# Attention denominators summed over partitions by accumulating DMAs and a small VectorE sum, in place of products with ones

## The chip, the cores and the metric

The kernel runs on one core of a Trainium2 chip. The metric is the device time of one execution in microseconds (us), lower being better. Every time below is a median of several executions. An execution is called slow when it is over 1.5% above the fastest of the same kernel. Each kernel with changes was run on the same chip and in the same rounds as the kernel before.

## The reference, cut to what matters

```python
B, H, S, D = 4, 8, 768, 64               # 16 clusters, d_model = H * D = 512
def attention(q, k, v, centroids):       # per batch and head
    q_assign = argmax(cos(q, centroids)); k_assign = argmax(cos(k, centroids))
    mask = q_assign[:, None] == k_assign[None, :]
    scores = where(mask, q @ k.T / sqrt(D), -1e9)
    e = exp(scores - max(scores))
    return (e / (sum(e) + 1e-9)) @ v
def hyena(x):                            # x: heads concatenated, [B, S, 512]
    x1, x2, x3 = split(x @ w_proj)
    y = x1 * irfft(rfft(x2, axis=1) * rfft(filter_fft, axis=0), axis=1) * x3
    return y @ w_out
```

`sum(e)` is the denominator that this case is about. The output is float32, [4, 768, 512].

## The kernel before

Work is done in 16 "head pairs" (two heads of one batch). For each of six key tiles of 128 keys TensorE makes scores, ScalarE turns them into `p` (exp), TensorE adds `p` times v into `pair`, and VectorE adds `p` into an accumulator `acc`, 128 partitions by 1,536. The keys lie on the partitions, so at the end of a head pair `acc` must still be summed over its 128 partitions. The kernel before does that with products with a block of ones, in four 32-column quadrants of the TensorE array:

```python
def den(e):
    for hp in range(2):
        for ch in range(2):
            z = 2 * hp + ch
            T.nc.tensor.matmul(ap(h)[32 * z:32 * z + 32, :384], T.ones32, T.acc[:, hp, ts(ch, 384)],
                               start=True, stop=True)
op(("PE", .68), den, te + 0.5, r=["acc", "ones"], w=[h], alloc=h, kind="den")
op(EV384, lambda e: copy(e, T.den, ap(h)[:, :384]), te + 1.5, r=[h], w=["den"], free=[h])
# 12 columns on each partition, by way of DRAM; then 1/x; then broadcast to all partitions
op(("SP", .6), ... dma_start(T.dd[os], T.den[0:128:32]), te + 2, r=["den"], w=[("dd", os)], byts=6e3)
op(("SP", .6), ... dma_start(T.dn, T.dd[os] ...), te + 4, r=[("dd", os)], w=["dn"], byts=6e3)
op(("DVE", .52), rec, te + 6, r=[], w=["dn"])                       # + eps, reciprocal
op(("SP", .6), ... dma_start(T.dr[os] ..., T.dn), te + 7, r=["dn"], w=[("dr", os)], byts=6e3)
for hp in range(2):
    op(("SP", .6), ... dma_start(T.rb[64 * hp:64 * hp + 64], T.dr[os][hp:hp + 1].to_broadcast([64, S])), te + 9, ...)
op(("DVE", 1.05), ... scalar_tensor_tensor(osv(), osv(), eps(), rbv(), ...), te + 12, ...)     # normalise
op({"ACT": .83, "DVE": .55}, ... copy(e, T.xT[xs][:, kt] ..., osv()), te + 13, ...)            # cast to bf16 xT
```

`xT` is what the projections of `hyena` read, so the whole chain from `den` to `xT` sets when they can start.

The code does not issue instructions directly. It makes a list of operations, each with an engine, a *modelled* duration, its inputs and a "due" time. A planner then simulates them and fixes one order for each engine, in which its instructions are issued. If an operation's input comes later than the model thought, the engine waits there, with everything planned after it: in the trace after (below) VectorE stood 6.59 us before one normalisation, and behind that ScalarE 4.90 and TensorE 4.52.

The softmax here doesn't subtract the row's maximum and nothing guards it: scores larger than these inputs give would overflow.

## Time and profile before

The kernel before takes 403.2 us (three executions, 401.54 to 403.23).

| | before |
|---|---|
| TensorE busy, share | 380.2 us, 95% |
| VectorE busy, share | 370.1 us, 92% |
| ScalarE busy, share | 275.5 us, 69% |
| share of TensorE in the chain that ended last | 81% |
| products with ones | 128 instructions |
| waits of the normalisation for its broadcast | 0.3 us |

First the page of its profile: the span, the busy time of each engine with its share of the span and its number of instructions, the granted TensorE clock and the DMA busy share in tenths for 40 slices of the span, the line of the software DMA queue (packets, MB, share of the 16 engines), and the chain of work that ended last.

```profile
span 401.3 us, 8872 instructions
PE 380.2 (95%) x3498; PEld 209.2 (52%) x3498; DVE 370.1 (92%) x513; ACT 275.5 (69%) x522; POOL 16.8 (4%) x55
...
PEclk9999999999999999999999999999999999999988
DMA  9939968127411433126521326014212001100304
...
q0 software_dynamic: 1056, 2.10, 3.0%
...
PE 81%; DVE 11%; ACT 4%; issue 2%; POOL 0%; DVEq 0%; POOLq 0%; ACTq 0%
```

TensorE (PE) is busy 95% and VectorE (DVE) 92%: two engines near their limit, with 21.1 us of TensorE idle in the whole span (401.3 − 380.2). Now some groups of instructions: line, engine, operation, tiles, shapes and count, then busy us and mean ns of one, then the engine's idle time just before them and what ended it.

```profile
L732 PE MATMUL bank<-acc,ones 128*32 128x384 f32 x128 | 13.6, 498 | 0.2 <-DVE acc L719 0.2
L780 DVE SCALAR_TENSOR_TENSOR osb<-osb,rb 128x768 f32<-128x768 f32 x15 | 15.2, 1013 | 0.3 <-DMA rb<-dr 0.3
L279 DVE CAST xT<-osb 128x768 bf16<-128x768 f32 x15 | 8.4, 560 | 0.5
```

The products with ones are 128 instructions. The normalisation (L780) waited 0.3 us for its broadcast in the whole run: the denominator chain is hidden. The timeline shows how well, for one head pair (start, duration, engine, line, operation). The reciprocal is followed at once by other work, and the normalisation comes 12.8 us later with no wait before it (there is no bracket at its end):

```profile
67.70 0.23 DVE L744 RECIPROCAL dn<-dn 128x12 f32<-128x12 f32 x1
...
80.54 1.01 DVE L780 SCALAR_TENSOR_TENSOR osb<-osb,rb 128x768 f32<-128x768 f32 x1
```

Finally the view by stretches of time, here two of its stretches: length, then busy us (and instructions) of PE, PE weight loads, DVE, ACT and POOL, then clock, DMA busy share and GB/s.

```profile
60.00:100.00 40.00, 39.08 (x322) 21.04 (x318) 34.95 (x40) 34.21 (x67) 0.00 (x0) 1.00 0.51 124
...
300.00:330.00 30.00, 29.93 (x280) 16.03 (x276) 29.44 (x40) 19.53 (x38) 0.00 (x0) 1.00 0.09 22
```

TensorE works almost without a gap in both, and the DMA engines have room, 0.51 and 0.09.

### The profile page before, as it was taken

The page shows a single profiled execution, that of the slowest core. Times are in us where ns is not written, and L with a number is a line of the kernel's source. Part 1 is how long each engine was busy: PE and PEld are TensorE (multiplying, and loading weights), DVE is VectorE, ACT ScalarE, POOL GpSimd, SP SyncE. Part 2 cuts the span into 40 slices and gives each one's busy share as a digit, 9 for nine tenths or more (in the row PEclk, how much of TensorE's full clock was granted, in tenths as well). Part 3 has the DMA queues.
Part 4 walks back from the last instruction along what each step waited for, and adds up shares of the span by engine and source line. Part 5 has one row for each costly group of instructions (what it writes and reads, how often), then busy time and mean ns, then how long its engine had stood idle before and what let it go on. Part 6 is the DMA issues. An engine that isn't in the chain of part 4 may idle for free.

```text
span 401.3 us, 8872 instructions
## 1 busy us (share of the span) xinstructions
PE 380.2 (95%) x3498; PEld 209.2 (52%) x3498; DVE 370.1 (92%) x513; ACT 275.5 (69%) x522; POOL 16.8 (4%) x55
## 2 busy tenths in 40 slices
PE   3979999999999999999999999999999999999963
PEld 2544554645545655554545655564555555555731
DVE  8899997989899999999899999997999999999981
ACT  4997888889855897676872877689865676523512
POOL 8700000000000000000000000000000000000000
PEclk9999999999999999999999999999999999999988
DMA  9939968127411433126521326014212001100304
GB/s 173 228 59 219 210 145 199 41 65 193 123 43 27 117 76 86 43 82 196 135 84 57 80 47 153 3 41 167 94 41 51 10 3 42 42 2 20 140 0 158
DMA packets 67233, 37.09 MB, mean 92 GB/s; under 512 B 56700, under 2 KB 62328, under 8 KB 67192
## 3 DMA queue, kind: packets, MB, share of 16 engines
q1 hardware_dynamic: 62856, 33.62, 32.5%
q0 software_dynamic: 1056, 2.10, 3.0%
q10 hardware_dynamic: 3280, 0.82, 1.2%
q8 instruction: 27, 0.44, 0.4%
q14 instruction: 14, 0.11, 0.1%
HBM read 30.66 MB, written 6.48 MB: 93 GB/s over the span
## 4 chain that ended last, share of the span: by engine, by line
PE 81%; DVE 11%; ACT 4%; issue 2%; POOL 0%; DVEq 0%; POOLq 0%; ACTq 0%
PE bank L63 30%; PE pair L709 29%; PE bank L817 5%; PE bank L674 4%; PE bank L570 3%; PE bank L732 3%; PE bank L599 3%; DVE acc L719 2%; PE bank L467 1%; PE bank L610 1%; ACT p L698 1%; DVE y L907 1%; PE bank L493 1%; DVE hm L454 1%; DVE yy L905 1%
## 5 line engine op out<-in xcount | busy, mean ns | idle before, releaser
L709 PE MATMUL pair<-p,vraw 128*64 128x385 f32 x768 | 143.3, 489 | 0.0
L698 ACT ACTIVATE p<-bank 128x512 f32<-128x512 f32 x192 | 114.2, 617 | 29.6 <-PE bank L63 25.3
L719 DVE TENSOR_TENSOR acc<-p,acc 128x1536 f32<-128x1536 f32 x64 | 111.9, 1748 | 4.0 <-ACT p L698 2.4
L709 PEld LDWEIGHTS pair<-p,vraw 128*64 128x64 f32 x768 | 53.6, 136 | 44.6 <-issue 37.9
L63 PE MATMUL bank<-aug,aug 128*64 128x512 bf16 (+3 forms) x610 | 69.1, 326 | 1.4 <-DVE aug L536 0.7
L695 ACT ACTIVATE p<-bank 128x512 f32<-128x512 f32 x96 | 58.8, 612 | 4.2 <-PE bank L63 3.1
L63 PE MATMUL bank<-xT,wpj 128*64 128x384 bf16 x512 | 51.9, 327 | 0.1
L63 PEld LDWEIGHTS <-aug 128*64 128x64 bf16 (+1 forms) x610 | 35.3, 109 | 30.2 <-issue 17.5
L63 PEld LDWEIGHTS <-wpj 128*64 128x64 bf16 x512 | 27.9, 109 | 22.3 <-issue 13.5
L277 ACT COPY qkT<-bank 128x384 f32<-128x384 f32 x58 | 27.2, 497 | 10.3 <-PE bank L63 9.3
L63 PEld LDWEIGHTS <-y 128*64 128x64 bf16 x448 | 22.4, 112 | 18.3 <-issue 6.9
L719 DVE TENSOR_TENSOR acc<-p,p 128x1536 f32<-128x1536 f32 x16 | 28.0, 1752 | 1.8 <-ACT p L698 1.5
L674 PE MATMUL bank<-aug,aug 80*128 80x256 bf16 (+1 forms) x120 | 28.6, 274 | 0.0
L63 PE MATMUL bank<-wout,y 128*64 128x512 bf16 x192 | 25.4, 402 | 3.3 <-DVE y L907 3.3
L841 DVE TENSOR_TENSOR tm<-bank,hm 128x512 f32<-128x512 f32 x44 | 27.7, 680 | 0.0
L570 PE MATMUL bank<-ident,qkraw 128*128 128x128 f32 x144 | 27.1, 275 | 0.0
L277 ACT CAST aug<-qkT 64x768 bf16<-64x768 f32 x30 | 24.9, 831 | 1.6 <-DVE qkT L279 1.0
L817 PE MATMUL bank<-wpj,xT 128*64 128x512 bf16 x192 | 22.1, 379 | 1.0 <-DVE xT L279 1.0
L277 ACT COPY ob<-bank 128x512 f32<-128x512 f32 x20 | 11.5, 589 | 15.0 <-PE bank L63 14.8
L570 PEld LDWEIGHTS bank<-ident,qkraw 128*128 128x128 f32 x144 | 18.3, 141 | 3.8 <-issue 2.1
L279 DVE CAST aug<-qkT 64x768 bf16<-64x768 f32 x30 | 16.6, 552 | 2.4 <-ACT qkT L277 1.7
L724 ACT COPY osb<-pair 128x770 f32<-128x770 f32 x16 | 12.8, 800 | 8.6 <-PE pair L709 8.3
(145 smaller groups left out, 436.8 us busy)
## 6 DMA issues: line engine op xcount, KB each, us to landing
vraw<-in_v_dram SPq DMA_DIRECT2D x16, 384.0 KB
qkraw<-in_q_dram SPq DMA_DIRECT2D x30, 192.0 KB
qkraw<-in_k_dram SPq DMA_DIRECT2D x30, 192.0 KB
rb<-dr SPq DMA_DIRECT2D x30, 192.0 KB
out_dram<-ob SPq DMA_DIRECT2D x11, 512.0 KB
y<-in_moe_filter_fft_dram SPq DMA_DIRECT2D x4, 384.0 KB
wpj<-in_moe_w_proj_dram POOLq DMA_DIRECT2D x1, 1536.0 KB, 12.8
aug<-ohT SPq DMA_DIRECT2D x60, 24.0 KB
```

The source lines that it names most:

```text
L63: tensor.matmul(out[64 * i:64 * i + 64], lhsT[:, 64 * i:64 * i + 64], rhs, start=start, stop=stop)
L277: T.nc.scalar.copy(out, in_)
L279: (T.nc.vector if e == "DVE" else T.nc.gpsimd).tensor_copy(out, in_)
L570: tr2 = [lambda i=i, s=s, h=h: T.nc.tensor.transpose(bank(h.ids[i // 3])[:, ts(i % 3, 128)], raw(s, i), T.ident) for i in range(NT)]
L674: T.nc.tensor.matmul(ap(h)[:, c:c + hi - lo], ag[1][:K, ts(sk, 128)], ag[0][:K, lo:hi], start=True, stop=True)
L695: T.nc.scalar.activation(o, ap(h).rearrange("p (a b) -> p a b", a=2), Act.Exp, scale=0.125)
L698: T.nc.scalar.activation(flat(s)[:, lo:lo + 512], ap(h), Act.Exp, scale=0.125)
L709: T.nc.tensor.matmul(o[64 * hp:64 * hp + 64, ch, :385], T.vraw[vs][:, hp, sk * D:(sk + 1) * D], T.p[slots[sk]][:, hp, 384 * ch:384 * ch + ...
L719: T.nc.vector.tensor_tensor(T.acc[:], P_(t[0]), P_(t[1]) if len(t) == 2 else T.acc[:], op=Alu.add)
L724: op(("ACT", .83), lambda e: T.nc.scalar.copy(T.osb[os], two(ob)[:, :, :385]), te, r=[ob], w=[("osb", os)], free=[ob])
L817: T.nc.tensor.matmul(ap(h)[64 * i:64 * i + 64], T.xT[xs][:, kt, c:c + 64], T.wpj[:, kt, DM:2 * DM], start=kt == 0, stop=kt == ND - 1)
L841: op(("DVE", .68), lambda e, i=i, cs=cs, r=r, h=h: T.nc.vector.tensor_tensor(T.tm[r][:, cs], ap(h), hmrow(i, (0, 2, 2, 3)[2 * r + cs]), op ...
```

## The change

The intent is to take the 128 products with ones off the busiest engine and give the sum over partitions to the DMA engines, which have room. For the first 14 of 16 head pairs three DMAs issued by GpSimd add the upper half of the partitions onto the lower half (64, then 32, then 16 rows of 6 KB). The 16 rows that remain are written to DRAM and read back so that each partition holds 12 columns of all 16 rows. One small VectorE reduction adds the 16. The accumulator is doubled, so that the next head pair can start.

The diff (541 lines), cut to its core. Cuts are marked with `...`.

```diff
-        h = Bank()
-        def den(e):
-            ... products with ones ...
+        late = n == NG - 1                       # the last two head pairs keep the products
...
+                flat_ = lambda: T.acc[os][:].rearrange("p a b -> p (a b)")
+                rows = 64
+                while rows >= ROWS:              # ROWS = 16
+                    op(("POOL", 1.0), lambda e, rows=rows: T.nc.gpsimd.dma_start(
+                        flat_()[:rows], flat_()[rows:2 * rows], accum_op=Alu.add), te, r=[], w=[("acc", os)],
+                       byts=rows * 12e3)
+                    rows //= 2
+                op(("SP", .6), ... dma_start(T.dd[os], flat_()[:ROWS]), te + 2, r=[("acc", os)],
+                   w=[("dd", os)], byts=98e3)
+                op(("SP", .6), ... dma_start(T.dp, T.dd[os].rearrange("r (p b) -> p r b", b=12)),
+                   te + 4, r=[("dd", os)], w=["dp"], byts=700e3)
+                def gather(e):
+                    T.nc.vector.tensor_reduce(T.dn, T.dp[:].rearrange("p r b -> p b r"), axis=AX, op=Alu.add)
+                    T.nc.vector.tensor_scalar(T.dn, T.dn, EPS * S, None, op0=Alu.add)
...
# the normalisation writes bf16 xT itself; the cast is gone
-            op(("DVE", 1.05), ... scalar_tensor_tensor(osv(), osv(), eps(), rbv(), ...
-        op({"ACT": .83, "DVE": .55}, lambda e: copy(e, T.xT[xs][:, kt]..., osv()), ...
+            op(("DVE", .6 if last else 1.05), ... scalar_tensor_tensor(xv()[:, a_], osv()[:, a_], eps(), ...
...
# products may use all 128 columns if the array is in that mode already; scores no longer woven with transposes
-MODES = {"pv": (64, 64), "score": (64, 64), "bc": (64, 64), "inv": (64, 64), "proj": (64, 64), ...
+MODES = {"pv": 64, "bc": 64, "half": 64, "sim": 32, "den": 32, "score": 0, "proj": 0, "inv": 0}
...
# the planner: a bandwidth for each queue instead of one for all; loads not before due - LEAD; new constants
-                s = max(o.end + 1.3, st.bw)
-                st.bw = s + o.byts / rate
-                o.end = st.bw + 0.6
+                s = max(o.end + 1.3, st.bw.get(e, 0.0))
+                st.bw[e] = s + o.byts / rate
+                o.end = st.bw[e] + 0.6
...
-    T0 = 10.36
-    TAU1 = 3.298
+    T0 = 9.692
+    TAU1 = 3.059
```

So the diff has two parts: the denominators, and "the rest": the direct write of `xT`, the array modes, the unwoven scores and the planner's changes.

## The prediction

> **What bounds the kernel.** The busy-time lines give TensorE 380.2 us of 401.3 (95%), VectorE 370.1 (92%), ScalarE 275.5 (69%). By stretches, from 60 to 350 us TensorE is busy 98 to 100%, VectorE 87 to 99%. The chain of waits is TensorE 81%, VectorE 11%. From 340.9 to 389.4 us the timeline shows VectorE without a gap: the tail is VectorE's. DMA is busy 83 to 93% until 60 us and 10 to 50% later.
>
> **Removed.** (1) 14 of 16 products with ones. In the TensorE timeline each lasts 0.78 us to the next start, and the group before takes 0.10 us longer than usual (1.40 after 1.30), since the array changes from 64 to 32 columns: 14 x 0.88 = 12.3 us. [...] (2) 14 denominator evictions: about 5 us ScalarE, 1 VectorE. (3) The normalisation writes bf16 xT directly; 16 casts go: 8.4 us VectorE, 0.8 ScalarE. (4) Scores woven with transposes. I count this as nothing: 3 scores with 6 transposes took 1.42 us woven; apart they take 0.65 + 0.80. (5) Score and projection products may stay in 128-column mode after a transpose: perhaps 5 to 20 of 124 mode changes saved, 0.5 to 2 us.
>
> **Added.** For 14 head pairs, three accumulating DMAs (64, 32, 16 partitions of 6 KB) issued by GpSimd, a 98 KB write, a read back in 48-byte pieces (2,048), and a VectorE reduction of 192 elements. A reduction of 384 took 0.555 us, so I estimate 0.36 us, 5 us in all. The accumulator is doubled. I guess a latency of 30 to 40 us to the normalisation; projections that need xT are placed later and the accumulator is rewritten only after some 25 us, so mostly it hides. [...] the trace has no accumulating DMA, so its speed is my largest unknown.
>
> **Critical path.** TensorE falls by about 13 us (380 to 367), nearly all in its saturated stretch. VectorE falls by 4 to 5 us (to about 365), ScalarE by 6. VectorE becomes co-limit and returns some of the gain; work that either engine may do will shift to ScalarE. I expect attention to end (last accumulation, 348.9 + 1.75 us) 7 to 9 us earlier, and the tail to shorten by 2 to 4 us, because more of the third batch's convolution fits before it and a cast leaves its chain. In sum about 11 to 12 us.
>
> **Predicted: 391.5 us, 8 in 10 between 385 and 399. Faster by over 2%: 0.76; within 2%: 0.20; slower: 0.04.**
>
> **What would show it.** Products with ones fall from 128 instructions to 16; TensorE busy 364 to 370, VectorE 362 to 368, both 92% or more of the span; no xT cast; a reduction group of about 0.36 us x14; the woven 256-column scores gone, some score products with 128 columns; software-queue packets up; no long wait of accumulator additions on a DMA; mode changes under 124.
>
> **What would make it wrong.** Accumulating DMAs slower than about 6 us each: the accumulator or xT comes late and TensorE waits. The software queue slowing VectorE, or delaying input loads before 100 us. VectorE already being the true limit, so that only 4 or 5 us come. Whole 128-column products slower than pairs of halves.

## More of the kernel before

The model of a DMA in the kernel before has one bandwidth for all queues:

```python
if o.byts:                              # a DMA
    s = max(o.end + 1.3, st.bw)         # st.bw: when the DMA engines are free, all queues together
    st.bw = s + o.byts / rate
    o.end = st.bw + 0.6
```

## The result

The changed kernel takes 423.0 us (four executions, 421.83 to 424.82) against 403.22 in the same rounds. The ratio is 1.0505, with a 95% interval from 1.0458 to 1.0551: slower by 5%. The predicted 391.5 us, and even the upper end of the range, 399, are far off. Ratios here and below are the mean time of one kernel's fast runs over that of the other's of the same rounds, so they are not quite the ratio of the medians quoted.

The page of the profile after:

```profile
span 421.4 us, 8556 instructions
PE 380.4 (90%) x3312; PEld 212.4 (50%) x3312; DVE 366.8 (87%) x507; ACT 276.4 (66%) x512; POOL 50.0 (12%) x95
...
PEclk9979999996999999999999999999996999989988
DMA  9939989858966984649985772454856211101203
...
q0 software_dynamic: 3296, 11.73, 19.7%
...
PE 52%; DVE 23%; DMA 13%; issue 5%; ACT 3%; SPq 2%; ACTq 1%; DVEq 0%
```

Three things are to be seen. First, TensorE is busy as long as before to within 0.2 us, although it runs 186 instructions fewer. Second, the clock line has new dips, a 7, two 6s and an 8 in the first 36 slices. Third, the chain that ended last is no longer a TensorE chain. DMA is 13% of it, and it was not in the list before.

TensorE's idle time grew from 21.1 to 41.0 us (421.4 − 380.4), by 19.9, which is the whole loss of 20.1 us of span. The removed work is there: counted from the trace's instructions, the products with ones fell from 10.2 to 1.3 us, and changes of array mode fell from 124 to 83, which at the prediction's 0.10 us each is 4.1 us (in the trace before, 8 products of `p` and v take 1.30 us to the next start when that product has 64 columns, 1.40 when it has 128 and 1.43 when it has 32: medians of 61, 17 and 12 groups). But there are 23.9 us of half clock between 15 and 385 us; before there was none. TensorE was busy for 18.4 us of them and so did 9.2 us less work, an estimate from half the rate: in one group of 8 products of `p` and v at half clock, the starts came 276 ns apart, at full clock 143 (median of 92 groups). The slow clock takes back most of the saving (−8.9 − 4.1 + 9.2 = −3.8; measured +0.2; where the other 4.0 us went was not separated), and the idle time comes on top.

Where does it arise? Groups of the profile after, with the idle time before them at the end:

```profile
L765 DVE SCALAR_TENSOR_TENSOR xT<-osb,rb 128x768 bf16<-128x768 f32 x15 | 15.2, 1014 | 11.4 <-DMA rb<-dr 11.2
L688 ACT COPY osb<-pair 128x770 f32<-128x770 f32 x16 | 12.8, 802 | 13.9 <-DVE xT L765 9.1
L729 DVE TENSOR_REDUCE dn<-dp 128x12 f32<-128x192 f32 x14 | 6.8, 485 | 0.0
```

The normalisation now waits 11.2 us for its broadcast `rb` (0.3 before). ScalarE in turn waits 9.1 us for the normalisation, because the copy out of `pair` needs the buffer `osb` that the normalisation reads. The view by stretches shows two places where this hurts:

```profile
60.00:100.00 40.00, 30.84 (x240) 15.44 (x236) 29.45 (x36) 29.48 (x55) 4.94 (x6) 0.97 0.77 140
...
300.00:330.00 30.00, 25.17 (x206) 13.73 (x204) 21.61 (x22) 19.17 (x37) 3.88 (x5) 0.89 0.60 104
```

From 60 to 100 us TensorE lost 8.2 us of busy time against before, from 300 to 330 it lost 4.8. The DMA share rose from 0.51 to 0.77 and from 0.09 to 0.60. The timeline of the second place shows a stall running through three engines (the bracket is the idle time before, and what ended it; SPq is the issue of a DMA on SyncE):

```profile
305.16 5.09 SPq L449 DMA_DIRECT2D aug<-ohT  x6
310.34 0.52 SPq L733 DMA_DIRECT2D dr<-dn  x1
310.91 1.14 SPq L449 DMA_DIRECT2D aug<-ohT  x2
314.02 1.12 SPq L736 DMA_DIRECT2D rb<-dr  x2
...
320.70 1.02 DVE L765 SCALAR_TENSOR_TENSOR xT<-osb,rb 128x768 bf16<-128x768 f32 x1 [6.59 <-DMA rb<-dr]
321.75 0.80 ACT L688 COPY osb<-pair 128x770 f32<-128x770 f32 x1 [4.90 <-DVE xT L765]
321.77 2.35 PE L795 MATMUL bank<-wpj,xT 128*64 128x512 bf16 x10 [4.52 <-DVE xT L765]
```

Read it from the top. The reciprocal was done at 308.78. Its write `dr` (L733) was issued only at 310.34, behind six mask copies issued before it on the same queue (305.16 to 310.25). The broadcasts `rb` went out from 314.02, beside a 64-row accumulate issued at 314.41, and the second landed at 320.6. The normalisation waited 6.59 us, ScalarE 4.90, TensorE 4.52. The clock was at half from 319.4 to 326.2 us. TensorE was busy for 4.4 us of that, so at half the rate it lost another 2.2 us of work. The granted clock in the intervals at half is 0.5, elsewhere 1.0, and between 15 and 385 us they last 3.4 or 6.8 us. How long TensorE must stand idle for one to come is not shown. At 319.4 us TensorE had stood idle for 2.1 us only, and in d_noacc (below) half clock at 65.8 us followed a gap of 1.79 us, while a gap of 2.74 us here, at 65.6 us, brought none.

The list of DMA issues has the new transfers (queue, count, KB each, median us from issue to landing):

```profile
acc<-acc POOLq DMA_DIRECT2D x14, 384.0 KB, 5.4
acc<-acc POOLq DMA_DIRECT2D x14, 192.0 KB, 4.0
...
acc<-acc POOLq DMA_DIRECT2D x14, 96.0 KB, 3.7
dd<-acc SPq DMA_DIRECT2D x14, 96.0 KB, 3.1
dp<-dd SPq DMA_DIRECT2D x14, 96.0 KB, 3.6
```

In the median each accumulate is under the 6 us that the prediction named as the danger; the longest took 10.7 us. The landings of one chain, with `dr` 2.7 and `rb` 3.8, add up to 26.3 us (5.4 + 4.0 + 3.7 + 3.1 + 3.6 + 2.7 + 3.8). The chain of the first head pair took 54 us, though, from 44.5 to 98.5 us in the timeline. Its second accumulate (issued 51.0) landed at 61.7, behind a 1,536 KB weight load issued on the same queue at 46.9. Its third went out only at 66.8, since the next head pair's first accumulate stood ahead of it in GpSimd's order and waited for VectorE until 66.3.

### The profile page after: what moved, and what is told of

Same layout as the page of the kernel before. It is cut to its first block, busy times and chain, and to the rows that moved or that the text cites. A ratio compares the mean times of both kernels' runs of the same rounds, so it can differ in the third digit from the quotient of the medians.

```text
span 421.4 us, 8556 instructions
## 1 busy us (share of the span) xinstructions
PE 380.4 (90%) x3312; PEld 212.4 (50%) x3312; DVE 366.8 (87%) x507; ACT 276.4 (66%) x512; POOL 50.0 (12%) x95
## 3 DMA queue, kind: packets, MB, share of 16 engines
q0 software_dynamic: 3296, 11.73, 19.7%
## 4 chain that ended last, share of the span: by engine, by line
PE 52%; DVE 23%; DMA 13%; issue 5%; ACT 3%; SPq 2%; ACTq 1%; DVEq 0%
PE pair L674 19%; PE bank L70 19%; DVE acc L684 7%; PE bank L795 4%; DMA rb<-dr 4%; DMA qkraw<-in_k_dram 3%; DVE tm L819 3%; DMA aug<-ohT 3%; PE bank L68 3%; PE bank L543 3%; DMA dr<-dn 2%; PE bank L571 2%; DVE aug L250 2%; DVE sd L876 1%; DVE xT L765 1%
## 5 line engine op out<-in xcount | busy, mean ns | idle before, releaser
L674 PE MATMUL pair<-p,vraw 128*64 128x385 f32 x768 | 146.3, 499 | 4.2 <-ACT osb L688 4.2
L70 PE MATMUL bank<-aug,aug 128*64 128x512 bf16 (+3 forms) x636 | 84.5, 329 | 2.7 <-DVE tm L819 0.6
L719 POOL DMA_DIRECT2D acc<-acc x42 | 33.3, 799 | 270.6 <-DVE acc L684 156.4
L70 PEld LDWEIGHTS <-aug 128*64 128x64 bf16 (+1 forms) x636 | 39.4, 110 | 40.2 <-issue 31.6
L70 PEld LDWEIGHTS <-wpj 128*64 128x64 bf16 x496 | 30.8, 109 | 16.3 <-issue 7.0
L248 ACT CAST aug<-qkT 64x768 bf16<-64x768 f32 x35 | 28.8, 830 | 1.3 <-DVE qkT L250 0.7
L684 DVE TENSOR_TENSOR acc<-p,p 128x1536 f32<-128x1536 f32 x16 | 28.0, 1752 | 1.1 <-ACT p L663 0.7
L765 DVE SCALAR_TENSOR_TENSOR xT<-osb,rb 128x768 bf16<-128x768 f32 x15 | 15.2, 1014 | 11.4 <-DMA rb<-dr 11.2
L543 PE MATMUL bank<-ident,qkraw 128*128 128x128 f32 x144 | 20.8, 280 | 3.1 <-DMA qkraw<-in_q_dram 2.7
L70 PE MATMUL bank<-wout,y 128*64 128x512 bf16 x144 | 19.6, 407 | 3.3 <-DVE y L885 3.3
L543 PEld LDWEIGHTS bank<-ident,qkraw 128*128 128x128 f32 x144 | 15.5, 140 | 11.8 <-issue 6.3
```

What stands on the lines that cost most here:

```text
L70: T.nc.tensor.matmul(out[64 * i:64 * i + 64], lhsT[:, 64 * i:64 * i + 64], rhs, start=start, stop=stop)
L248: T.nc.scalar.copy(out, in_)
L543: T.nc.tensor.transpose(bank(h.ids[i // 3])[:, ts(i % 3, 128)], raw(s, i), T.ident)
L674: T.nc.tensor.matmul(o[64 * hp:64 * hp + 64, ch, :385], T.vraw[vs][:, hp, sk * D:(sk + 1) * D], T.p[slots[sk]][:, hp, 384 * ch:384 * ch + ...
L684: T.nc.vector.tensor_tensor(T.acc[os], P_(t[0]), P_(t[1]) if len(t) == 2 else T.acc[os], op=Alu.add)
L719: op(("POOL", 1.0), lambda e, rows=rows: T.nc.gpsimd.dma_start(flat_()[:rows], flat_()[rows:2 * rows], accum_op=Alu.add), te, r=[], w=[("a ...
```

## The experiments

There were two readings at first. One says that the accumulating DMAs are to blame, either because the sums come late or because their traffic delays everything else. The rival says that the other parts of the diff, which the prediction took as neutral or better, make a worse order. The kernels that were made wrong compute something else but keep shapes and timing; each is named as such. Differences "to before" are those of the medians of the same rounds.

| kernel | median us | before, same rounds | difference | ratio, 95% interval |
|---|---|---|---|---|
| a_ones | 419.73 | 401.76 | +18.0 | 1.0434 (1.0380 to 1.0488) |
| b_dma | 442.28 | 401.76 | +40.5 | 1.0996 (1.0930 to 1.1062) |
| d_noacc (wrong) | 407.74 | 401.76 | +6.0 | 1.0126 (1.0068 to 1.0185) |
| d2_nodep (wrong) | 421.92 | 401.76 | +20.2 | 1.0479 (1.0394 to 1.0564) |
| a_shared | 409.10 | 403.57 | +5.5 | 1.0134 (1.0106 to 1.0163) |
| after_shared | 445.43 | 403.57 | +41.9 | 1.1037 (1.0999 to 1.1075) |
| b_queues | 412.01 | 403.57 | +8.4 | 1.0201 (1.0161 to 1.0241) |
| b_direct | 410.25 | 403.57 | +6.7 | 1.0173 (1.0143 to 1.0203) |
| b_traffic | 405.16 | 402.94 | +2.2 | 1.0054 (1.0000 to 1.0107) |
| after_real (three fast executions) | 425.89 | 402.94 | +23.0 | 1.0593 (1.0540 to 1.0646) |
| noacc_planned (wrong) | 402.81 | 402.94 | −0.1 | 1.0007 (0.9947 to 1.0067) |
| c_later | 422.94 | 402.94 | +20.0 | 1.0485 (1.0431 to 1.0539) |
| noacc_half (wrong) | 397.39 | 402.67 | −5.3 | 0.9865 (0.9822 to 0.9909) |
| b_half (wrong) | 399.90 | 402.67 | −2.8 | 0.9927 (0.9888 to 0.9966) |
| after_pool | 438.52 | 402.67 | +35.9 | 1.0865 (1.0815 to 1.0915) |

Differences of a few us are read here only where the interval excludes 1; those of b_traffic and noacc_planned do not.

### a_ones: everything but the accumulating DMAs

The changed kernel, with products with ones for all head pairs.

```diff
-        late = n == NG - 1
+        late = True
-            h, den_ = Bank(), lambda: T.sim[:, pr]
+            h, den_ = Bank(), lambda: T.acc[os][:, 0, :384]
...
```

> The changed kernel with only the denominators put back: all 16 head pairs use products with ones (their sums kept in the accumulator's own tile), everything else of the diff stays. Theory 1 (the accumulating-DMA chain is late, in-order engines wait for it[...]): 388 to 400 us, granted clock back at 0.985 or more, no VectorE wait on the broadcast of reciprocals over 1 us. Rival 2 (the rest of the diff is slow: unwoven transposes, 128-column products, new planning constants): 415 us or more.

It took 419.73 us, 18.0 more than before. So the rest of the diff alone, without one accumulating DMA, loses nearly as much as the whole change. The waits of VectorE (what waited, for what, us in total, times, longest) and the timeline name the place:

```profile
DVE dn L732 <- DMA dn<-dd: 6.7, 3, 5.6
```

```profile
64.93 0.23 DVE L732 RECIPROCAL dn<-dn 128x12 f32<-128x12 f32 x1 [5.61 <-DMA dn<-dd]
...
65.81 0.90 PE L543 MATMUL bank<-ident,qkraw 128*128 128x128 f32 x3 [5.16 <-DVE hm L425]
```

VectorE waits 5.61 us for a small read, TensorE waits 5.16 us behind it, and the clock is at half from 62.9 to 69.7 us. The read is late: of the first of eight mask copies, issued at 46.4 us, the last packet ended only at 55.9, after a 1,536 KB weight load from GpSimd's queue (44.3 to 55.6); the denominators' write stood behind the eighth mask on SyncE's queue and went at 59.4. So the run met the rival's expectation and missed the one of the reading that blames the DMAs of the sums, 388 to 400 us.

### b_dma: the kernel before with the accumulating DMAs

The denominators of the diff put into the kernel before, with the doubled accumulator and the planner's separate queues; its array modes, woven scores, casts and constants stay.

```diff
-        op(("PE", .68), den, te + 0.5, r=["acc", "ones"], w=[h], alloc=h, kind="den")
+        ... while rows >= ROWS: gpsimd.dma_start(..., accum_op=Alu.add); dd, dp, tensor_reduce, as in the diff ...
-                s = max(o.end + 1.3, st.bw)
+                s = max(o.end + 1.3, st.bw.get(e, 0.0))
```

> The kernel before with only the denominators changed to accumulating DMAs (14 of 16 pairs; accumulator doubled, centroid scratch moved into another tile to make room, the planner's DMA model with one bandwidth per queue). Theory 1: slower than before, 408 to 430 us, with waits on the broadcast of reciprocals and dips of the granted clock. Rival 2: 388 to 398 us, since 12 us of TensorE work are gone and the slow rest of the diff is absent.

It took 442.28 us, 40.5 more than before and more than either expectation allowed. Put into the kernel before, the accumulating DMAs lose twice as much as the whole diff. Something in the rest of the diff makes them more bearable; its constants are the likely part, but that was not tested alone. The parts cannot simply be added.

### d_noacc and d2_nodep: without the accumulates, and with them but not waiting for their sums

Both keep the changed kernel's planned order. d_noacc does not issue the 42 accumulating DMAs. d2_nodep issues them, but the next step of the chain reads a weight tile, so the chain does not wait for the sums. Both give wrong results.

```diff
 # d_noacc
-                    op(("POOL", 1.0), lambda e, rows=rows: T.nc.gpsimd.dma_start(
-                        flat_()[:rows], flat_()[rows:2 * rows], accum_op=Alu.add), te, r=[], w=[("acc", os)],
+                    op(("POOL", 1.0), lambda e: None, te, r=[], w=[("acc", os)],
 # d2_nodep
-                op(("SP", .6), lambda e: T.nc.sync.dma_start(T.dd[os], flat_()[:ROWS]), te + 2, ...
+                op(("SP", .6), lambda e: T.nc.sync.dma_start(
+                    T.dd[os], T.wpj[:ROWS, :2].rearrange("p a b -> p (a b)").bitcast(F32)), te + 2, ...
```

> The changed kernel in the same planned order, but the 42 accumulating DMAs are not issued (result wrong on purpose: 16 of 128 partitions summed; 1.0 added so that it stays finite). Theory 1: the chain is 12 to 25 us shorter, so 392 to 405 us, VectorE's 11 us of waits on the broadcast nearly gone. Rival 2: 417 us or more. Rival 3 (not the chain's lateness but the 10 MB of extra DMA traffic delays masks and loads): also fast, so this run does not tell 1 from 3.

> The changed kernel in the same planned order with all 42 accumulating DMAs issued, but the write of the 16 partial rows reads a constant weight tile instead of the accumulator, so that nothing in the chain waits for them (result wrong on purpose). Theory 1 (lateness): as fast as the run without accumulating DMAs, within 4 us, 392 to 407 us. Rival 3 (traffic): as slow as the changed kernel, 415 us or more. In between: both.

d_noacc took 407.74 us, d2_nodep 421.92. The first lies between the ranges that were expected; the second is what the reading that blames the traffic expected. Issuing the accumulates costs 14.2 us; that the chain waits for their sums adds nothing that can be seen (d2_nodep is 20.2 over before, the changed kernel 19.8, each in its own rounds). The waits of VectorE in d2_nodep look like those of the changed kernel although nothing in that chain waits for a sum:

```profile
DVE xT L766 <- DMA rb<-dr: 11.9, 7, 5.2
```

In d_noacc the wait for `rb` is 0.8 us:

```profile
DVE xT L764 <- DMA rb<-dr: 0.8, 1, 0.8
```

From 300 to 330 us TensorE was busy 29.75 of 30 us in d_noacc and 26.50 in d2_nodep:

```profile
300.00:330.00 30.00, 29.75 (x269) 20.27 (x265) 28.41 (x40) 16.18 (x32) 0.00 (x0) 1.00 0.23 46
```

```profile
300.00:330.00 30.00, 26.50 (x210) 14.70 (x208) 21.15 (x24) 17.49 (x34) 3.87 (x5) 0.89 0.52 95
```

So it is not a long chain of late sums. It is that other small transfers land later when the accumulates are in flight. For the head pair of the stall above, the time from the reciprocal to the landing of the second `rb` was 5.4 us in d_noacc, 9.7 in d2_nodep and 11.3 in the changed kernel, by the end of its last packet; the median of the 14 pairs was 5.8, 7.0 and 6.8. So most pairs lose about 1 us and a few lose much. The changed kernel and d_noacc also have one plan, so the time at which TensorE has done the same work can be compared. The changed kernel falls 4.5 us further behind between 60 and 80 us of work (the stall near 97 us), 6.9 between 250 and 280 (the stall near 320), and 2.6 in all the rest.

Two rivals that the prediction named can be put aside by the traces. The software queue did not slow VectorE: an addition into `acc` took 1,750 ns (median) before and 1,752 after. And whole 128-column score products are not slower in themselves: one of 512 columns takes 220 ns to the next start (noacc_planned, below), two halves 217 (before).

The next runs asked how, and what in the rest of the diff costs 18 us.

### a_shared and after_shared: the planner's one bandwidth again

a_ones and the changed kernel, each with the old DMA model in the planner.

```diff
-        st = SimpleNamespace(pool=0.0, dve=0.0, bw={}, ...
+        st = SimpleNamespace(pool=0.0, dve=0.0, bw=0.0, ...
-                s = max(o.end + 1.3, st.bw.get(e, 0.0))
-                st.bw[e] = s + o.byts / rate
-                o.end = st.bw[e] + 0.6
+                s = max(o.end + 1.3, st.bw)
+                st.bw = s + o.byts / rate
+                o.end = st.bw + 0.6
```

> The kernel of run a_ones (diff without the denominators, 419.7 us), with one more piece of the diff undone: the planner's DMA model has again one bandwidth for all queues together, not one for each. Theory 4 (that optimistic model orders VectorE, TensorE and SyncE so that in the DMA-saturated first 100 us they wait for small transfers): 402 to 412 us, the 5.6 us wait of the reciprocal on its read-back and the 5.2 us TensorE gap near 60 us gone. Rival 5 (the loss of the rest of the diff is that any re-planned order is worse than the tuned one, or sits in the product modes and pacing constants): within 4 us of 419.7, or slower.

> The changed kernel with only the planner's DMA model put back to one bandwidth for all queues, so that it counts the accumulating DMAs and the weight loads against the loads, masks and reciprocals. Theory 4: 400 to 414 us, VectorE's 11 us of waits on the broadcast of reciprocals down to under 4. Rival 5: 418 us or more.

a_shared took 409.10 us, 5.5 over before and in the range expected, where a_ones was 18.0 over: the planner's separate bandwidths are worth about 12 us of the loss. after_shared took 445.43 us, 41.9 over before, where the theory of the bandwidths had expected 400 to 414 in all. The changed kernel books each accumulate at 12 KB for a row of 6 KB and the read back at 700 KB for 98. With one bandwidth for all, those bookings should push every transfer late in the model; after_real, below, tests that. The two parts of the diff thus lean on each other.

### b_queues: only the separate bandwidths, in the kernel before

The opposite edit, and nothing else, in the kernel before.

> The kernel before with only the planner's DMA model changed to one bandwidth per queue. Theory 4: slower than before by 4 to 14 us (406 to 416 us), lost before 110 us. Rival 5 with the loss in product modes or pacing constants: within 3 us of before; rival 5 with any re-planning being worse: also slower, but the loss not confined to the first 110 us.

It took 412.01 us, 8.4 more, with the same work to do, as its expectation said. VectorE's waits:

```profile
DVE dn L743 <- DMA dn<-dd: 6.8, 1, 6.8
```

One wait, ending at 63.15 us, then half clock from 64.7 to 71.5 us. In the table of work done over time (time at which TensorE had done so many us of work, the denominators left out, minus that of before), the loss is one step: +2.9 at 30 us of work, +10.7 at 40, +8.8 at 70, and +8.6 at 330. So a plan with a bandwidth for each queue, against one bandwidth for all, lost 8.4 us in one kernel and some 12 in the other. How transfers of several queues run beside each other was not measured here.

### b_direct: only the direct write of xT, in the kernel before

```diff
-            op(("DVE", 1.05), ... scalar_tensor_tensor(osv(), osv(), eps(), rbv(), ...), w=[("osb", os)], lock=True)
+            op(("DVE", 1.05), ... scalar_tensor_tensor(xv(), osv(), eps(), rbv(), ...), w=[("xT", xs, kt)], lock=True)
-        op({"ACT": .83, "DVE": .55}, lambda e: copy(e, T.xT[xs][:, kt] ..., osv()), ...)
```

> The kernel before with only one piece of the diff: the normalisation writes bf16 xT directly and the 16 casts are gone. VectorE busy falls by 8 us. If VectorE co-limits: 396 to 401 us. If TensorE alone limits: 400 to 403 us. If any re-planned order is worse than the tuned one: 404 us or more, in spite of less work.

It took 410.25 us, 6.7 more, for less work. In the table of work over time it stands within 0.8 us of before up to 310 us of work (361 us of time), then falls back: +4.0 at 320 and +7.7 at 330. So the loss is in the last part alone, where the planner chose another order. VectorE's busy time fell only to 367.9 us (370.1 before), since the planner gave it other work for the casts. The run shows two things: taking the casts off VectorE gave nothing until 361 us, and a new plan can lose several us by itself. Why the tail's new order is worse was not settled.

### b_traffic: only the traffic, with the order unchanged

The kernel before in its own order, with 42 accumulating DMAs on a scratch tile (rows of 5 KB), issued when a head pair's output is copied. Nothing waits for them.

```diff
+                T.nc.gpsimd.tensor_copy(T.scr[0:1, 0:1], T.osb[os][0:1, 0, 0:1])
+                for rows in (64, 32, 16):
+                    T.nc.gpsimd.dma_start(T.scr[:rows], T.scr[rows:2 * rows], accum_op=Alu.add)
```

> The kernel before, in its own unchanged order, plus three accumulating DMAs (64, 32, 16 rows of 5 KB, 83% of the change's bytes) for each of 14 head pairs on an unused scratch tile, started when the pair's output is copied; nothing waits for them and the result stays correct. If the traffic by itself is what costs the changed kernel its 14 us: 410 us or more. If it costs only where the order leaves no slack before a small transfer's reader: 402 to 406 us, with landings of masks, loads and broadcasts slower by 0.3 to 1 us.

It took 405.16 us, 2.2 more (interval of the ratio 1.0000 to 1.0107), as expected for an order with slack. The small reads did land later: the median from the issue of `dn<-dd` to the end of its last packet rose from 1.6 to 2.3 us, that of `rb` only from 2.6 to 2.7. But in this order `xT` and `dn` have slack, and VectorE waited only 2.3 us for `rb` in all. So a similar traffic (83% of the bytes, at other moments, and the profile is of the slowest of four executions) costs about 2 us in an order with slack and 14 us in the changed kernel's.

### after_real, noacc_planned and c_later: three attempts at a better plan

after_real is after_shared with the bytes that the DMAs really move. noacc_planned is after_real with the accumulates neither planned nor issued (wrong): what the change would be worth if the sum were free. c_later is the changed kernel with the normalisation held back in the plan.

```diff
 # after_real, besides the one bandwidth of after_shared
-                       byts=rows * 12e3)
+                       byts=rows * 6e3)
-                   te + 4, r=[("dd", os)], w=["dp"], byts=700e3)
+                   te + 4, r=[("dd", os)], w=["dp"], byts=98e3)
 # noacc_planned, besides after_real
-                    op(("POOL", 1.0), ... gpsimd.dma_start(..., accum_op=Alu.add) ...
 # c_later
+            if o.kind == "norm":
+                o.ready = max(o.ready, o.due + LATER)        # LATER = 26.0
```

> The changed kernel planned with one bandwidth for all queues (as in after_shared) but with the real bytes of the accumulating DMAs and of the gather (6 KB per row and 98 KB, where the diff books 12 KB and 700 KB). Theory: after_shared was slow (445 us) because these doubled and sevenfold bytes then pushed the planned loads and masks too late; so 400 to 416 us. If sharing itself is bad for this chain: 430 us or more.

> As after_real, but the accumulating DMAs are neither planned nor issued (result wrong on purpose: 16 of 128 partitions summed, 1.0 added). It is the changed kernel with the products gone for free. If the three parts add (rest of the diff +18.0, of it 10.6 undone by the shared model; products -12.0; traffic +14.2 not paid): 401.8 + 18.0 - 10.6 - 12.0 = 397 us, within 4. If VectorE gives the gain back: 402 us or more.

> The changed kernel with the normalisation of the first 14 pairs planned at least 38 us after its pair's scores, where the planner had it as soon as its modelled transfers allow. If the in-order wait of VectorE for the broadcast (11.2 us, four times) costs what it shows and its clock dips: 405 to 416 us, that wait under 3 us. If the output buffer (two, reused after two pairs) then blocks ScalarE and TensorE instead: 418 us or more, with waits of the output copy on the normalisation.

after_real took 425.89 us in its three fast executions: honest bytes help against after_shared by 19 us (+23.0 and +41.9), but it is no better than the changed kernel. This expectation was missed. VectorE waited 5.4 us for `rb` in it, under half of the changed kernel's 11.2, so that wait alone does not set the time of every plan. noacc_planned took 402.81 us, a tie with before. That is short of the 397 us that adding up the parts gave, and is the time expected if VectorE gives the gain back. It has no half clock between 15 and 385 us, TensorE is busy 375.0 us and VectorE 363.8. So even a free sum, with this diff, gains nothing against before. c_later took 422.94 us; VectorE still waited 9.3 us for `rb`. ScalarE's output copy waited 8.5 us for the normalisation, as the second expectation said. Holding the operation back in the plan moved other work, but hardly the wait, so it says little about slack.

### noacc_half and b_half: is VectorE the limit that swallowed the gain?

noacc_planned and the kernel before, each with 64 of the 80 additions into `acc` done on half the columns, which takes about 51 us of VectorE work away (both wrong).

```diff
-                    T.nc.vector.tensor_tensor(T.acc[os], P_(t[0]), P_(t[1]) if len(t) == 2 else T.acc[os], op=Alu.add)
+                    T.nc.vector.tensor_tensor(*[x[:, :, :S if len(t) == 2 else 384] for x in (
+                        T.acc[os][:], P_(t[0]), P_(t[1]) if len(t) == 2 else T.acc[os][:])], op=Alu.add)
```

> noacc_planned in its own order, with 64 of the 80 accumulator additions on half of their columns: about 51 us less VectorE work, TensorE's work unchanged (result wrong on purpose, 1.0 added to stay finite). If VectorE is the co-limit that keeps the removed products from paying: 385 to 396 us against 402.8. If TensorE alone limits: 399 us or more.

> The kernel before in its own order with the same halving of VectorE's additions (result wrong on purpose). If TensorE is the sole limit before, as its 95% and the null effect of the direct write up to 310 us suggest: 397 to 402 us, the gain in the last 60 us. If VectorE co-limits before too: 386 to 396 us.

noacc_half fell to 397.39 us, 5.4 under noacc_planned (from other rounds), between its two expectations; b_half to 399.90 us, 2.8 under before, as expected if TensorE alone limits. So with TensorE lightened, VectorE does hold back some of the gain. But even with 51 us of VectorE work gone, the two kernels differ by 2.5 us only, where the removed products and casts promise more. The rest is open.

### after_pool: the end of the chain on GpSimd's queue

The changed kernel with `dr` and `rb` issued by GpSimd, so that they need not stand behind the masks on SyncE's queue.

```diff
+            q, nq = ("SP", T.nc.sync) if late else ("POOL", T.nc.gpsimd)
-            op(("SP", .6), lambda e: T.nc.sync.dma_start(T.dr[os]..., T.dn), ...
+            op((q, .8), lambda e: nq.dma_start(T.dr[os]..., T.dn), ...
-                op(("SP", .6), lambda e, hp=hp: T.nc.sync.dma_start(T.rb[...
+                op((q, .8), lambda e, hp=hp: nq.dma_start(T.rb[...
```

> The changed kernel with the last three transfers of the denominators (reciprocals out, two broadcasts back) of the first 14 pairs issued on GpSimd's queue, not behind masks and loads on SyncE's. If that queue is why the broadcast is late: 405 to 417 us, VectorE's wait on it under 5 us. If the accumulating transfers now stand before them in GpSimd's queue and on the engines: 420 us or more.

It took 438.52 us, worse than the changed kernel by about 16 (+35.9 and +19.8), as the second expectation said. VectorE's wait for `rb` rose to 18.3 us, and GpSimd's issue of `rb` waited 21.0 us, in 11 waits, for `dr` to land:

```profile
POOL rb L737 <- DMA dr<-dn: 21.0, 11, 5.2
```

No correct version that was tried beats the kernel before.

## Why the prediction was wrong

What held:

- The removed work was real. Products with ones fell from 128 instructions to 16, casts of `xT` are gone, mode changes fell from 124 to 83, VectorE's busy time was 366.8 us (362 to 368 predicted), software-queue packets rose from 1,056 to 3,296, and accumulator additions wait for a DMA 0.3 us in all.
- The size of the gain from the products was about right in one place. From a_ones to d_noacc, which has the rest of the new chain but no accumulate, the time falls by 12.0 us; the prediction had 12.3. The two have different plans, and in another pair (a_shared to noacc_planned) the fall is 5.6 us, so the figure depends on the plan.

What failed, in the order of the sum, in us over before:

1. "The rest" was counted as a small gain: 0.5 to 2 us for array modes, nothing for the unwoven scores, and nothing at all for the planner, which the prediction did not name. It measured +18.0 (a_ones). About 12 of that is the planner's bandwidth for each queue (a_shared), which alone costs 8.4 in the kernel before (b_queues). This is the largest error of the prediction.
2. The products come out: −12.0, to +6.0 (d_noacc).
3. "So mostly it hides" said the prediction of the new chain's latency. Issuing the accumulates costs +14.2 us, to +20.2 (d2_nodep). The dependence on their sums adds nothing that can be seen (+19.8 for the changed kernel). The prediction looked for the cost in the accumulates themselves ("slower than about 6 us each"). They took 5.4, 4.0 and 3.7 us in the median, and the cost came through other transfers: `dr` late behind masks on SyncE's queue (issued 1.56 us after the reciprocal's end in the stall near 320 us), and `rb` beside accumulates in flight (longest landing 7.0 us, 5.5 in d_noacc).
4. "TensorE busy 364 to 370" failed, at 380.4, mostly by the 23.9 us of half clock, 17.1 of which came with TensorE gaps of 4.2, 4.5 and 3.4 us. TensorE lost 9.2 us of work by it (the estimate above), against 13.0 removed; the other 4.0 us were not separated. The prediction had no term for it. Both shares of the span fell below the promised 92%, to 90 and 87.
5. ScalarE did not fall by 6 us but stayed at 276.4, since it took over other work (casts of `aug` alone rose from 24.9 to 29.0 us), as the prediction itself had said of work that either engine may do.
6. The reduction took 0.485 us, not 0.36, together 1.8 us more on VectorE. That matters little.

The prediction did name two ways to be wrong that came true, a late `xT` and the software queue in the way of loads, but gave "slower" a chance of 0.04.

How much the parts add up must be read with care. b_dma (+40.5) and after_shared (+41.9) show that parts interact. Each kernel that changes the list of operations has a new order as a whole, and b_direct shows that this can be worth 6.7 us. The steps from d_noacc to d2_nodep to the changed kernel have one plan and are the cleanest. Open stays why noacc_planned, with 9 us of products' busy time and 8 us of casts gone, only ties with before (TensorE's busy time fell by only 5.2 us): VectorE explains part of it (noacc_half), and the order and other waits were not separated. Open is also what bookings in the planner would make the accumulating DMAs pay. The array modes, the unwoven scores and the new constants were not tested one by one (5.5 us are left in a_shared), and whether the transfers come late by what stands before them on their queue or by the accumulates in flight was not separated.

## What to carry to other kernels

In this kernel, whose order is fixed in advance, work moved to DMA cost little by its traffic and much by what then landed late. Before moving such work, list what stands before the small transfers on their queues (here six masks before `dr`), and how much slack their consumers have (b_traffic +2.2 us with slack; 14.2 in the changed kernel's order). Read a diff of a planner's model as a change of the whole kernel, and test it alone first. With two engines above 90%, taking work from one was worth less here than its busy time, and a few stalls of 3 to 7 us took it all back, since half clock came with them: with three of the four TensorE gaps over 2 us between 15 and 385 us in the changed kernel (4.2, 4.5 and 3.4 us, not 2.7), for 6.8, 6.8 and 3.4 us.

## What the runs showed of DMA landings and of the clock

- An accumulate inside SBUF, issued on GpSimd's queue, took 5.4, 4.0 and 3.7 us from issue to landing for 384, 192 and 96 KB (medians of 14 each in the changed kernel), in a loaded system: the DMA share was 0.62 between 15 and 385 us.
- With accumulates in flight the median landing of a 192 KB broadcast rose from 3.5 us (d_noacc) to 3.8 (the changed kernel) and its longest from 5.5 to 7.0; a 6 KB read rose from 1.6 to 2.3 us to its last packet (b_traffic). With a 1,536 KB weight load in flight, a 24 KB mask copy took about 12 us (47.9 to 60 us in the changed kernel).
- The granted clock was 0.5 or 1.0, at half mostly for 3.4 or 6.8 us, once for 10.2 in after_pool. The length of a TensorE gap did not by itself tell whether half clock came. Gaps of 1.79 us in d_noacc (at 65.8 us), 1.95 in b_dma (at 133.4) and 2.12 in after_pool (at 137.4) came just before half clock; one of 2.74 us in the changed kernel (at 65.6) did not. Gaps of 4.2, 4.5 and 3.4 us there came with half clock of 6.8, 6.8 and 3.4 us.
- In the trace before, 8 products of `p` and v took 1.40 us in place of 1.30 to the next start when that product had 128 columns and not 64 (1.43 with 32), so a change of array mode there cost 0.10 to 0.13 us.
